# Last matrix product of an attention and two-layer kernel: 1280 of 2304 tokens by Strassen's seven products

## The chip, the cores and the metric

The kernel runs on one core of a Trainium2 chip. The metric is the device time of one execution in microseconds (us). Its engines are named as in the profile: PE (TensorE, the matrix unit; PEld are its weight loads), DVE (VectorE), ACT (ScalarE), POOL (GpSimd) and SP (SyncE, which here only issues the DMA transfers, in one queue and in order).

## The reference

```python
def reference(**kw):
    attn_out = _attn_ref(**attn_kwargs)          # 4 x 8 heads, 576 positions, 64 wide, causal
    x = attn_out.transpose(0, 2, 1, 3).reshape(2304, 512)
    x = _moe_ref(x=x, **moe_kwargs)              # 512 -> 2048 -> 512, leaky ReLU
    return _moe2_ref(x=x, **moe2_kwargs)

def _moe2_ref(x, w_in, w_out):
    h = x @ w_in                                 # 2304 x 512 @ 512 x 2048
    g = h * np.clip(h + 3.0, 0.0, 6.0) / 6.0
    return (g @ w_out).astype(np.float32)        # 2304 x 2048 @ 2048 x 512
```

The change concerns the last line alone: out = g @ w_out for 2304 tokens.

## The kernel before

The program is one long stream of matmuls on PE in stages: attention, the first pair of products (`w_in1`, `w_out1`), the product with `w_in2`, and the product with `w_out2`. Each fp32 factor is split into a high part, rounded to a narrower format that PE reads, and a low part that holds the rest (`split`: ACT copies the high part, line 160; DVE subtracts it, line 161). A product of two factors is then three matmuls: high by high, high by low, low by high.

The product with `w_in2` (line 879) already uses Strassen's form with seven products (the table `FORMS`). It runs over four groups of 576 tokens and eight steps j per group, and writes g to the HBM tensor `g_d` (named `g_scratch` in the profile), with 2048 rows (features) and 2304 columns (tokens).

The last stage (line 1042) reads g back in blocks of 512 tokens: four blocks of 512 and one of 256. For each of the 16 chunks f of 128 features it has a tile `gr` with two chunks (one DMA, line 1032, four buffers), the split of one chunk into `gh` and `gl` (three buffers each), and for each of the block's 128-token tiles three matmuls: gh or gl is the stationary factor (128 by 128), and the chunk of `w_out2` (`wo2[f]`, 512 columns) is the moving one. So a chunk takes 12 matmuls of 512 columns, a block 192. The sum over the chunks stays in one PSUM bank for each token tile; ACT scales it by 1/6 into `ot` (line 1052), and SP stores it.

The weights of this stage come in as 64-bit numbers that must be turned into fp32 on the chip first. `to_f32` does that for one chunk of 512 columns in five operations that depend on each other: ACT line 142, POOL line 144, POOL line 147, DVE line 152, DVE line 155. `split` then makes `wo` (ACT line 160, DVE line 161). `split_out` calls both, through two small buffers (`Spare`, the two halves of the tile `wo51`). Raw weights and results lie in the memory of `w_in2` pieces that are no longer needed (`places`). During the `w_in2` stage, `split_out` is called as soon as a raw chunk is there; the rest are called in the first block of the last stage, one for every second chunk.

The order on each engine is set when the program is built: a scheduler places the instructions by their priority, and each engine then goes through its own list strictly in order. An instruction whose data is late holds up all that stands behind it on that engine.

Of the kernel before, what the change touches and what calls it, by code (L numbers as in the profile page):

```python
# [61 lines left out]
def attention_moe_moe(ctx, tc, qt, kt, kq2, kqs, vs4, vp, s, w_in1, w_out1, alpha, w_in2, w_out2, out):  # L62
# [33 lines left out]
    def stage(**kw):  # L96
        roles.update(kw)
# [153 lines left out]
    def rows_of(p, n):  # L251

        out_, end = [], p + n
        while p < end:
            if p < B * NA:
                b, r = divmod(p, NA)
                m, t = min(end - p, NA - r), b * S + r
            else:
                b, r = divmod(p - B * NA, NQB)
                m, t = min(end - p, NQB - r), b * S + NA + r  # L260
            out_.append((t, m))
            p += m
        return out_
# [684 lines left out]
    wo2, outs = [], []  # L948

    places = []  # L950
    for j in range(4):
# [2 lines left out]
            places.append((f"wo{j - 1}1", j))  # L954
    places += [("wo31", 3), ("wo11", 3)]

    def load_out(f):

        t = wp.tile([P, CH, 2], U32, tag=places[f][0], name="wraw")
# [18 lines left out]
    with ExitStack() as ph2:  # L978
        cv = Spare()
        m5s = wp.tile([P, 2, NX2], F32, tag="wo71", name="m5")  # L980
        m2 = ph2.enter_context(tc.tile_pool(name="moe2", bufs=2))
        xbs = ExitStack()
        xb = xbs.enter_context(tc.tile_pool(name="xb", bufs=1))
        stage(a=[6, 1, 2], b=[0, 4, 5], c=[7, 3])
        xs[1] = load_x(xb, 1)
        last = None
        for i, (g, j) in enumerate(order):
            if i in (1, 3, 5):
                with tc.high_priority(offset=WLP):
# [28 lines left out]
        stage(o=[2, 5, 7, 0, 6, 3, 4, 1])
        NB2 = 512
        GC = 2  # L1020
        blocks = [(t0, min(NB2, NT - t0)) for t0 in range(0, NT, NB2)]
        for bi, (t0, n) in enumerate(blocks):
            ntt = n // P
            op = [bank("o") for i in range(ntt)]
            for f in range(FC):
                if bi == 0 and f < 2:
                    load_out(len(outs))
                if bi == 0 and len(wo2) < FC and f % 2 == 0:
                    split_out(len(wo2))
                if f % GC == 0:  # L1030
                    gr = gp.tile([P, GC, NB2], F32, tag="gr", bufs=4, name="gr")
                    nc.sync.dma_start(
                        gr[:, :, :n], g_d[f * P : (f + GC) * P, t0 : t0 + n].rearrange("(k p) t -> p k t", p=P)
                    )
                gh = gp.tile([P, NB2], F32R, tag="gh", bufs=3, name="gh2")
                gl = gp.tile([P, NB2], F32R, tag="gl", bufs=3, name="gl2")
                split(gh[:, :n], gl[:, :n], gr[:, f % GC, :n])
                wh, wl = wo2[f]
                for i in range(ntt):
                    tsl = slice(i * P, (i + 1) * P)  # L1040
                    for lt, r in ((gh, wh), (gh, wl), (gl, wh)):
                        nc.tensor.matmul(  # L1042
                            op[i], lt[:, tsl], r, start=(f == 0 and r is wh and lt is gh), stop=(f == FC - 1 and lt is gl)
                        )
            for i in range(ntt):
                ot = stg.tile([P, DM], F32, tag="yt", name="ot")
                halves = 2 if bi == len(blocks) - 1 else 1
                w = DM // halves
                for c in range(halves):
                    cols = slice(c * w, (c + 1) * w)  # L1050
                    if c == 0:
                        nc.scalar.activation(ot[:, cols], op[i][:, cols], AF.Copy, scale=1.0 / 6.0)
                    else:
                        nc.vector.tensor_scalar(ot[:, cols], op[i][:, cols], 1.0 / 6.0, 0.0, op0=ALU.mult, op1=ALU.add)
                    at = 0
                    for t, m in rows_of(t0 + i * P, P):
                        nc.sync.dma_start(out[t : t + m, cols], ot[at : at + m, cols])
                        at += m
# [37 lines left out]
```

## Time and profile before

| | |
|---|---|
| time, median of 3 runs | 1000.36 us (999.53 to 1003.92) |
| the profiled execution's own time | 1005.35 us |
| its span (first to last instruction) | 1003.6 us |
| PE busy | 980.6 us (98%) |
| DVE, ACT, POOL busy | 613.7, 632.2, 439.6 us |
| last matmul of the `w_in2` product ends, last stage alone on PE | about 812.7 us |
| last matmul of the last stage ends | about 999.0 us |

A row of the profile says which engine ran which line on which tile, for how long, and what ended the idle time before it. Matmuls are pipelined, so a row's duration for one matmul is longer than the distance to the next; distances between starts are what add up.

### The profile page before, as it was taken

To read this page: it belongs to the slowest core of one execution; us is meant where nothing else is said; L and a number is where in the kernel's file an instruction comes from. 1 tells how busy PE (TensorE), PEld (TensorE's weight loads), DVE (VectorE), ACT (ScalarE), POOL (GpSimd) and SP (SyncE) were. 2 spreads that over 40 slices of the span, in tenths; PEclk is the share of its full clock that TensorE was granted. 3 is DMA by queue.
4 is the path that set the end of the run, shared out by engine and by line. 5 is a ranking of instruction groups with operands and counts; after the bars stand their busy time and mean duration, and the time that the engine had idled before them with its cause. 6 is when DMAs were issued, how large, how long until landed. Compare 5 with 4: busy or idle time off the path is not lost.

```text
span 1003.6 us, 18109 instructions
## 1 busy us (share of the span) xinstructions
PE 980.6 (98%) x6218; PEld 880.8 (88%) x6218; DVE 613.7 (61%) x1504; ACT 632.2 (63%) x1434; POOL 439.6 (44%) x587
## 2 busy tenths in 40 slices
PE   8789999999999999999999999999999999999998
PEld 5568788999999998998998888999999988888886
DVE  5778885466666666766563895886658774222222
ACT  6568778678768778778764664766656653232322
POOL 5654666667666666666642763542202230000000
PEclk9779999999999999999999999999999999999999
DMA  6990014113122222213104421524248843443422
GB/s 212 300 361 1 24 30 128 45 46 91 52 76 74 58 69 83 67 52 97 52 14 153 122 94 63 194 107 150 111 158 289 280 153 116 116 147 86 145 62 85
DMA packets 60436, 114.47 MB, mean 114 GB/s; under 512 B 6056, under 2 KB 22744, under 8 KB 60344
## 3 DMA queue, kind: packets, MB, share of 16 engines
q1 hardware_dynamic: 60344, 113.32, 34.9%
q8 instruction: 49, 0.80, 0.3%
q14 instruction: 43, 0.35, 0.1%
HBM read 84.84 MB, written 28.46 MB: 113 GB/s over the span
## 4 chain that ended last, share of the span: by engine, by line
PE 92%; ACT 3%; DVE 2%; issue 1%; DMA 1%; POOL 1%; SPq 0%; DVEq 0%; POOLq 0%; ACTq 0%
PE h L248 20%; PE y L675 20%; PE o L1042 20%; PE a L879 10%; PE b L879 5%; PE s L410 4%; PE pv L472 4%; PE pt L447 4%; PE c L879 2%; PE s L322 1%; PE pv L603 1%; PE pt L593 1%; PE h L534 1%; DMA wraw<-in_w_in 1%; DMA gr<-g_scratch 1%
## 5 line engine op out<-in xcount | busy, mean ns | idle before, releaser
L248 PE MATMUL h<-xhi,wi 128*128 128x256 f32 (+1 forms) x896 | 228.3, 323 | 2.8 <-DVE gt L698 1.5
L1042 PE MATMUL o<-wo,gh 128*128 128x512 f32 x576 | 174.7, 389 | 0.0
L248 PEld LDWEIGHTS h<-xhi,wi 128*128 128x128 f32 x896 | 157.4, 192 | 16.4 <-DVE gt L698 1.9
L675 PE MATMUL y<-gh,wo 128*128 128x256 f32 (+1 forms) x896 | 162.0, 315 | 0.0
L248 PE MATMUL h<-xlo,wi 128*128 128x256 f32 (+1 forms) x448 | 143.7, 321 | 0.0
L675 PEld LDWEIGHTS y<-gh,wo 128*128 128x128 f32 x896 | 133.8, 190 | 11.2 <-ACT gh L701 0.4
L161 DVE TENSOR_TENSOR gl<-gr,gh 128x512 fp32r<-128x512 f32 (+1 forms) x80 | 51.1, 640 | 126.6 <-ACT gh L160 111.9
L1042 PEld LDWEIGHTS o<-wo,gh 128*128 128x128 f32 x576 | 107.9, 188 | 22.1
L160 ACT ACTIVATE gh<-gr 128x512 fp32r<-128x512 f32 (+1 forms) x80 | 46.8, 588 | 112.4 <-PE o L1042 109.7
L879 PE MATMUL a<-x,wc 128*128 128x288 f32 x768 | 113.2, 295 | 0.7 <-ACT z L886 0.7
L144 POOL TENSOR_SCALAR wcv<-wcv 128x512 f32<-128x512 f32 x64 | 47.7, 752 | 146.5 <-ACT wcv L142 142.4
L1042 PE MATMUL o<-wo,gl 128*128 128x512 f32 x288 | 109.5, 389 | 0.0
L879 PEld LDWEIGHTS a<-x,wc 128*128 128x128 f32 x768 | 106.0, 188 | 1.5 <-ACT z L886 1.2
L675 PE MATMUL y<-gl,wo 128*128 128x256 f32 (+1 forms) x448 | 91.6, 317 | 0.0
L248 PEld LDWEIGHTS h<-xlo,wi 128*128 128x128 f32 x448 | 86.3, 193 | 5.9
L422 POOL TENSOR_SCALAR t<-t,rec 128x384 f32<-128x384 f32 (+2 forms) x96 | 65.6, 686 | 57.3 <-DVE rec L421 32.9
L413 DVE CUSTOM_DVE_ANT_0 t<-s,mask 128x384 f32<-128x384 f32 (+2 forms) x96 | 53.4, 562 | 56.4 <-PE pt L447 34.4
L698 DVE SCALAR_TENSOR_TENSOR gt<-gt,beta,h 128x256 f32<-128x256 f32 (+1 forms) x112 | 61.7, 552 | 34.0 <-ACT gt L697 32.8
L418 ACT ACTIVATE t<-t,m 128x384 f32<-128x384 f32 (+2 forms) x96 | 67.2, 700 | 17.2 <-DVE m L413 15.8
L675 PEld LDWEIGHTS y<-gl,wo 128*128 128x128 f32 x448 | 69.7, 190 | 6.0 <-issue 0.2
L702 POOL TENSOR_TENSOR gl<-gt,gh 128x256 fp32r<-128x256 f32 x80 | 59.3, 743 | 31.4 <-ACT gh L701 29.5
L701 ACT ACTIVATE gh<-gt 128x256 fp32r<-128x256 f32 (+1 forms) x112 | 53.1, 477 | 29.5 <-DVE gt L698 27.9
(136 smaller groups left out, 2014.2 us busy)
## 6 DMA issues: line engine op xcount, KB each, us to landing
g_scratch<-gt SPq DMA_DIRECT2D x64, 288.0 KB
wraw<-in_w_in SPq DMA_DIRECT2D x32, 512.0 KB
wraw<-in_w_out SPq DMA_DIRECT2D x32, 512.0 KB
gr<-g_scratch SPq DMA_DIRECT2D x32, 512.0 KB
kraw<-in_kt SPq DMA_DIRECT2D x32, 288.0 KB
qraw<-in_qt SPq DMA_DIRECT2D x32, 160.0 KB
vraw<-in_vp SPq DMA_DIRECT2D x32, 160.0 KB
y_scratch<-yt SPq DMA_DIRECT2D x18, 256.0 KB
```

The source lines that it names most:

```text
L144: keep(nc.gpsimd.tensor_scalar(cf, cf, W_MOST, -W_MOST, op0=ALU.min, op1=ALU.max))
L161: keep(nc.vector.tensor_tensor(lo, of, hi.bitcast(F32), op=ALU.subtract))
L248: nc.tensor.matmul(dst, lt, r, start=first and i == 0, stop=last and i == len(terms) - 1)
L413: nc.vector.tensor_tensor_reduce(t[:n, a:e], sc[:n, : e - a], mask[:n, MASK + n - (e - a) :][:, : e - a] if e == w else mask[:n, : e - a], ...
L418: nc.scalar.activation(t[:n, :w], t[:n, :w], AF.Exp, bias=m[-1][:n], scale=-1.0, accum_out=den[:n])
L422: nc.gpsimd.tensor_scalar(t[:n, :w], t[:n, :w], rec[:n], 1.0, op0=ALU.mult, op1=ALU.mult)
L675: nc.tensor.matmul(ys[dc // per][:, o : o + n], which[:, dc * P : (dc + 1) * P], gg, start=(f == 0 and which is wl and dc % per == 0), sto ...
L698: nc.vector.scalar_tensor_tensor(gt, gt, beta[:, f : f + 1], hp[:, :n], op0=ALU.mult, op1=ALU.add)
L701: nc.scalar.activation(gh, gt, AF.Copy)
L702: (nc.vector if n == 512 else nc.gpsimd).tensor_tensor(gl, gt, gh.bitcast(F32), op=ALU.subtract)
L879: nc.tensor.matmul(dst[:, :NX2], lt, r, start=first and n == 0, stop=n == len(terms) - 1, skip_group_check=not first,)
L1042: nc.tensor.matmul(op[i], lt[:, tsl], r, start=(f == 0 and r is wh and lt is gh), stop=(f == FC - 1 and lt is gl))
```

## The change

The last stage is cut in two. The first 1024 tokens (two blocks of 512) go on as before, three buffers for `gr` in place of four, and the chunks are taken in the order 0, 8, 1, 9, ... (`chunks`), so that the two halves of the feature dimension come in pairs j. The other 1280 tokens are five blocks of 256 tokens. For them the product of each pair (2 by 128 tokens, 2 by 128 features, 2 by 256 columns) is made by Strassen's seven products instead of eight: 7 times 3 matmuls of 256 columns for each of the eight j. A block has four steps (`steps`, two j each).

What that needs besides matmuls:

- `make_forms(j)`, once for each j, placed in the two plain blocks: four differences of weights on DVE (line 1058, 256 columns each), split into new tiles `wf2` (two times ACT line 160 and DVE line 161, 512 columns). They need the whole fp32 weights. For j from 4 to 7 `split_out` now writes the converted weights straight into a kept tile (`direct`, through `Half`); for j from 0 to 3 DVE adds the high and low parts again (line 1054, two times 512 columns).
- `left_forms`, once for each of the 20 steps: two DMAs of 256 KB into `gq` (two buffers, line 1072), four sums and differences on DVE (lines 180 to 183, 256 columns each), and the split of `gq` (1024 columns) into `ga` and of the sums (768 columns) into `gs`. It is called one step ahead.
- `close`, once for each block: two copies on ACT, five operations on DVE (line 1104), two on POOL (lines 1110 and 1111), and the stores.

The kept tiles for j = 4 to 7 lie in memory that the last step of the `w_in2` product still uses (`slots[NJ + j]`), and only eight chunks of `w_out2` instead of all that are there are converted during that stage (`FC // 2`).

```diff
+    wo2, outs = {}, []
+    chunks = [j + h * NJ for j in range(NJ) for h in range(2)]
+    slots = [f"{nm}{j}{i}" for j in range(4, NU) for nm in ("wi", "wo") for i in range(2)]
+    slots.append(slots.pop(slots.index("wo51")))
+    direct = {}
...
+    def split_out(k):
+
+        f = chunks[k]
+        pool = cv
+        if k >= FC // 2:
+            j = f % NJ
+            if j not in direct:
+                direct[j] = wp.tile([P, 2, CH], U32, tag=slots[NJ + j], name="wf")
+            pool = Half(direct[j][:, f // NJ])
+        (cf,) = to_f32([outs[k]], pool, "wcv", 2, lambda ins: ins, (False,))
...
-                if len(wo2) < len(outs) - 1:
+                if len(wo2) < min(len(outs) - 1, FC // 2):
...
+        def make_forms(j):
+
+            if j in direct:
+                wf = direct[j].bitcast(F32)
+            else:
+                wf = gp.tile([P, 2, CH], F32, tag="wf", bufs=1, name="wf")
+                for h in range(2):
+                    hi, lo = wo2[j + h * NJ]
+                    nc.vector.tensor_tensor(wf[:, h], hi.bitcast(F32), lo.bitcast(F32), op=ALU.add)
+            tt = fp.tile([P, 4, ND], F32, tag="s", name="tt")
+            b11, b12, b21, b22 = (wf[:, h, c * ND : (c + 1) * ND] for h in range(2) for c in range(2))
+            for dst, x, y in ((0, b12, b11), (1, b22, tt[:, 0]), (2, b22, b12), (3, b21, tt[:, 1])):
+                nc.vector.tensor_tensor(tt[:, dst], x, y, op=ALU.subtract)
...
+        def left_forms(t0, jp):
+
+            gq = fp.tile([P, 2, 2, NS], F32, tag="gq", name="gq")
+            for h in range(2):
+                c = (h * NJ + 2 * jp) * P
+                nc.sync.dma_start(gq[:, h], g_d[c : c + 2 * P, t0 : t0 + NS].rearrange("(j p) t -> p j t", p=P))
+            sf = fp.tile([P, 3, 2, P], F32, tag="s", name="sf")
+            quads = [gq[:, h, :, m * P : (m + 1) * P] for h in range(2) for m in range(2)]
+            s_forms(nc.vector, *quads, [sf[:, i] for i in range(3)])
+            ga = fp.tile([P, 2, 2, 2, NS], F32R, tag="ga", name="ga")
+            split(ga[:, 0], ga[:, 1], gq)
+            gs = fp.tile([P, 2, 3, 2, P], F32R, tag="gs", name="gs")
+            split(gs[:, 0], gs[:, 1], sf)
...
+        ORDER = (1, 6, 5, 7, 2, 3, 4)
...
+        made = {(0, 6): 0, (0, 11): 1, (1, 0): 2, (1, 3): 3, (1, 5): 4, (1, 7): 5, (1, 9): 6, (1, 11): 7}
...
+                if (bi, k) in made:
+                    make_forms(made[bi, k])
+                if k % GC == 0:
+                    gr = gp.tile([P, GC, NB2], F32, tag="gr", bufs=3, name="gr")
...
+        for at, (t0, jp) in enumerate(steps):
+            if at + 1 < len(steps):
+                ahead.append(left_forms(*steps[at + 1]))
+            of = ahead.pop(0)
...
+                for k, i in enumerate(ORDER):
+                    a, b = FORMS[i - 1]
+                    (ah, al), (bh, bl) = of(a, jj), forms[j][b]
+                    for x, (lt, r) in enumerate(((ah, bh), (ah, bl), (al, bh))):
+                        tc.keep_in_program_order(
+                            nc.tensor.matmul(
+                                acc[i], lt, r, start=(j == 0 and x == 0 and k % 2 == 0),
```

How the lists of the engines change shows best at three places.

The first is on DVE, in the first plain block, up to the ninth chunk's weights, `wo_10920` in the changed kernel (in the kernel before, the ninth chunk's are `wo_10754`). The names: `wcv` and `wf` are weights under conversion, `gl2` the low part of a chunk of g, `tt` differences of weights, `wf2` their split. Before, the rows from the last conversion of chunks 8 and 9 on:

```order
L152 SCALAR_TENSOR_TENSOR wcv_8671<-wcv_8671,wraw_10453 128x512 [waits Pool_49]
L152 SCALAR_TENSOR_TENSOR wcv_8671<-wcv_8671,wraw_10455 128x512 [waits DMAHW7_49,Pool_49]
L155 SCALAR_TENSOR_TENSOR wcv_8671<-wraw_10453,wcv_8671 128x512 [waits DVE_49]
L155 SCALAR_TENSOR_TENSOR wcv_8671<-wraw_10455,wcv_8671 128x512 [waits DVE_49]
L161 TENSOR_TENSOR wo_10754<-wcv_8671,wo_10754 128x512 [waits Activation_49]
L893 SCALAR_TENSOR_TENSOR gt_10843<-gt_10843,a_10757 128x288 [waits Activation_49]
L161 TENSOR_TENSOR wo_10824<-wcv_8671,wo_10824 128x512 [waits Activation_49]
L161 TENSOR_TENSOR gl2_10998<-gr_10979,gh2_10997 128x512 [waits PE_49,Activation_49]
L889 TENSOR_TENSOR m5_8672<-a_10827,m5_8672 128x288 [waits PE_49]
```

Now, the last rows before the ninth chunk's weights are whole:

```order
L152 SCALAR_TENSOR_TENSOR wf_11199<-wf_11199,wraw_10912 128x512 [waits DMAHW0_49,Pool_49]
L161 TENSOR_TENSOR gl2_11154<-gr_11151,gh2_11153 128x512 [waits DMAHW2_49,PE_49,Activation_49]
L1058 TENSOR_TENSOR tt_11172<-wf_11169,tt_11172 128x256 [waits DVE_49]
L155 SCALAR_TENSOR_TENSOR wf_10914<-wraw_10453,wf_10914 128x512 [waits DVE_49]
L155 SCALAR_TENSOR_TENSOR wf_10914<-wraw_10455,wf_10914 128x512 [waits DVE_49]
L155 SCALAR_TENSOR_TENSOR wf_11199<-wraw_10912,wf_11199 128x512 [waits DVE_49]
L161 TENSOR_TENSOR wo_11148<-wf_11100,wo_11148 128x512 [waits Activation_49]
L1058 TENSOR_TENSOR tt_11172<-wf_11169,tt_11172 128x256 [waits DVE_49]
L161 TENSOR_TENSOR wf2_11177<-tt_11172,wf2_11177 128x512 [waits Activation_49]
L161 TENSOR_TENSOR wo_10920<-wf_10914,wo_10920 128x512 [waits Activation_49]
```

Before, `wo_10754` stands ahead of the last gate rows of the `w_in2` product (the next row of line 889 reads `a_10827`, that product's last step). Now the low part of `wo_10920` stands 32 rows behind that product's last DVE row (line 893 on `a_10811`), after the conversions of the other seven kept chunks and the weight differences of the first two j, and `gl2_11154`, a tile of the eleventh chunk, ahead of it.

The second place is PE, where the eighth chunk ends and the ninth begins. Before and now:

```order
L1042 MATMUL o_10924<-wo_10684,gh2_11081 128x512 x2
L1042 MATMUL o_10924<-wo_10684,gl2_11082 128x512
L1042 MATMUL o_10921<-wo_10754,gh2_11107 128x512 [waits Activation_49]
L1042 MATMUL o_10921<-wo_10754,gh2_11107 128x512
L1042 MATMUL o_10921<-wo_10754,gl2_11108 128x512 [waits DVE_49]
```

```order
L1145 MATMUL o_10911<-wo_10684,gl2_11085 128x512
L1145 MATMUL o_10908<-wo_10920,gh2_11111 128x512 [waits Activation_49]
L1145 MATMUL o_10909<-wo_10920,gh2_11111 128x512
L1145 MATMUL o_10910<-wo_10920,gh2_11111 128x512
L1145 MATMUL o_10911<-wo_10920,gh2_11111 128x512
L1145 MATMUL o_10908<-wo_10920,gh2_11111 128x512 [waits DVE_49]
```

The ninth chunk's first four matmuls now need the high part of `wo_10920` from ACT, and the fifth its low part from DVE; before, the waits there were for g alone.

The third place is one step of the Strassen blocks, which has nothing like it before: DVE's rows, and SP's two rows for the buffer that `ga_12038` gives free (`gq_12142` takes the memory of `gq_12030`; its first DMA waits on DVE).

```order
L161 TENSOR_TENSOR ga_12038<-gq_12030,ga_12038 128x1024 [waits Activation_49]
L181 TENSOR_TENSOR sf_12089<-sf_12089,gq_12086 128x256 [waits DVE_49]
L182 TENSOR_TENSOR gq_12086<-gq_12086 128x2x128
L183 TENSOR_TENSOR sf_12089<-gq_12086,sf_12089 128x256 [waits DVE_49]
L161 TENSOR_TENSOR gs_12097<-sf_12089,gs_12097 128x768 [waits Activation_49]
L180 TENSOR_TENSOR sf_12145<-gq_12142 128x256 [waits DMAHW1_49,DMAHW0_49]
L161 TENSOR_TENSOR ga_12094<-gq_12086,ga_12094 128x1024 [waits Activation_49]
```

```order
L1072 DMA gq_12142<-g_scratch 128x2x256 [waits DMAHW5_49,DMAHW4_49,DVE_49]
L1072 DMA gq_12142<-g_scratch 128x2x256
```

So between the rows of `ga` of two steps stands one row, line 180, that needs the DMA which the earlier of the two lets start.

## Rows read from the trace of the kernel before

**Rows 1.** The page: busy time, share of the span, instructions.

```profile
PE 980.6 (98%) x6218; PEld 880.8 (88%) x6218; DVE 613.7 (61%) x1504; ACT 632.2 (63%) x1434; POOL 439.6 (44%) x587
```

**Rows 2.** Chain that ended last, from 805 us: start, length, what.

```profile
812.07 0.79 PE a L879 x6
812.86 186.15 PE o L1042 x821
...
999.03 0.39 ACT ot L1052
```

**Rows 3.** Stretches: busy us and count of PE, PEld, DVE, ACT, POOL; clock; DMA.

```profile
812.70:999.03 186.33, 186.33 (x824) 154.15 (x822) 56.62 (x91) 57.91 (x101) 5.47 (x8) 1.00 0.37 112
```

**Rows 4.** PE in order of time, 256-column matmuls: start, us, operation, count.

```profile
199.83 1.00 PE L675 MATMUL y<-gh,wo 128*128 128x256 f32 x7
200.67 0.64 PE L675 MATMUL y<-gl,wo 128*128 128x256 f32 x4
201.15 0.28 PE L248 MATMUL h<-xhi,wi 128*128 128x256 f32 x1
```

**Rows 5.** DVE in order of time, around the last `w_in2` matmul.

```profile
809.88 0.76 DVE L893 SCALAR_TENSOR_TENSOR gt<-gt,z 128x576 f32<-128x576 f32 x1 [0.40 <-ACT gt L892]
...
813.60 0.45 DVE L893 SCALAR_TENSOR_TENSOR gt<-gt,a 128x288 f32<-128x288 f32 x1
813.97 0.69 DVE L161 TENSOR_TENSOR wo<-wcv,wo 128x512 fp32r<-128x512 f32 x1
...
820.79 1.29 DVE L152 SCALAR_TENSOR_TENSOR wcv<-wcv,wraw 128x512 uint32<-128x512 uint32 x2
821.99 1.29 DVE L155 SCALAR_TENSOR_TENSOR wcv<-wraw,wcv 128x512 uint32<-128x512 uint32 x2
823.20 0.69 DVE L161 TENSOR_TENSOR gl<-gr,gh 128x512 fp32r<-128x512 f32 x1
```

**Rows 6.** Groups by shape from 600 us: busy, mean ns, idle before.

```profile
L161 DVE TENSOR_TENSOR x<-yr,x 128x1152 fp32r<-128x1152 f32 x6 | 8.1, 1352 | 4.5 <-ACT x L160 4.5
L161 DVE TENSOR_TENSOR gl<-gr,gh 128x256 fp32r<-128x256 f32 x16 | 6.7, 425 | 18.5 <-ACT gh L160 10.1 <-PE o L1042 8.4
L161 DVE TENSOR_TENSOR x<-yt,x 128x864 fp32r<-128x864 f32 x6 | 6.3, 1050 | 0.0
```

**Rows 7.** ACT and POOL in order of time: gate, conversion and split.

```profile
812.90 0.51 ACT L892 ACTIVATE gt<-a,three 128x288 f32<-128x288 f32 x1 [1.75 <-PE a L879]
...
815.17 0.66 ACT L142 ACTIVATE wcv<-wraw 128x512 f32<-128x512 f32 x1
...
822.77 1.23 ACT L160 ACTIVATE wo<-wcv 128x512 fp32r<-128x512 f32 x2
...
815.91 0.63 POOL L144 TENSOR_SCALAR wcv<-wcv 128x512 f32<-128x512 f32 x1 [5.92 <-ACT wcv L142]
817.55 1.72 POOL L147 TENSOR_SCALAR wraw<-wcv 128x512 f32<-128x512 f32 x2
```

**Rows 8.** PE waits and the granted clock (last figure but two).

```profile
48.15:54.97 6.82, 4.42 (x18) 3.34 (x19) 6.72 (x12) 2.66 (x7) 1.36 (x2) 0.50 0.98 268
54.97:65.21 10.24, 7.46 (x42) 5.05 (x40) 7.74 (x33) 7.29 (x25) 5.21 (x10) 1.00 1.04 407
170.00:180.00 10.00, 8.44 (x70) 8.03 (x69) 4.07 (x16) 9.78 (x30) 9.41 (x16) 1.00 0.45 125
...
50.55 0.69 PE L603 MATMUL pv<-pT,vraw 128*64 128x256 f32 x2 [4.11 <-DVE pT L597]
174.65 0.39 PE L248 MATMUL h<-xhi,wi 128*128 128x256 f32 x1 [1.54 <-DVE gt L698]
```

**Rows 9.** GB/s in 40 slices of 2.6 us from a 256 KB `gr` issue, then 3.5 us from a 512 KB one.

```profile
GB/s 0 0 0 0 0 0 0 0 0 0 0 0 0 0 0 79 95 110 110 126 79 79 110 189 221 236 347 362 378 347 299 299 174 110 126 110 32 16 0 0
GB/s 0 0 0 0 0 0 0 0 0 0 0 117 117 140 140 23 140 47 70 187 140 187 281 304 421 374 421 421 398 398 398 398 328 258 164 70 47 0 0 0
```

**Rows 10.** Chain at the start of the `gr` loads: landing of the first of four.

```profile
783.46 5.23 DMA gr<-g_scratch
```

More of the change, by code (lines that the diff above doesn't have):

```diff
@@ L955, in attention_moe_moe, with load_out, __init__, tile @@
     places += [("wo31", 3), ("wo11", 3)]
-    def load_out(f):
-        t = wp.tile([P, CH, 2], U32, tag=places[f][0], name="wraw")
+    def load_out(k):
+        f = chunks[k]
+        t = wp.tile([P, CH, 2], U32, tag=places[k][0], name="wraw")
         tc.keep_in_program_order(nc.sync.dma_start(t.rearrange("p f t -> p (f t)"), w_out2[f * P : (f + 1) * P, :].bitcast(U32)))
         outs.append(t)
-    def split_out(f):
-        (cf,) = to_f32([outs[f]], cv, "wcv", 2, lambda ins: ins, (False,))
-        t = wp.tile([P, 2, CH], F32R, tag=places[f][0], name="wo")
+    class Half:
+        def __init__(self, of):
+            self.of = of
+        def tile(self, *args, **kw):
+            return self.of
+    def split_out(k):
+        f = chunks[k]
+        pool = cv
[5 more added lines that the diff above has]
+        (cf,) = to_f32([outs[k]], pool, "wcv", 2, lambda ins: ins, (False,))
+        t = wp.tile([P, 2, CH], F32R, tag=places[k][0], name="wo")
         split(t[:, 0], t[:, 1], cf)
-        wo2.append((t[:, 0], t[:, 1]))
+        wo2[f] = (t[:, 0], t[:, 1])
     A1, B1 = 3, 4
@@ L1017, in attention_moe_moe @@
         right.close()
[L1018 to L1023, printed above, removed]
+        fp = late.enter_context(tc.tile_pool(name="forms", bufs=2, side="right"))
+        NB2, NS, GC = 512, 256, 2
+        ND = DM // 2
+        plain = (0, NB2)
+        rest = range(2 * NB2, NT, NS)
+        forms = []
+        def make_forms(j):
[10 more added lines that the diff above has]
+                nc.vector.tensor_tensor(tt[:, dst], x, y, op=ALU.subtract)
+            t = []
+            for i in range(2):
+                hl = wp.tile([P, 2, 2, ND], F32R, tag=slots[2 * j + i], name="wf2")
+                split(hl[:, 0], hl[:, 1], tt[:, 2 * i : 2 * i + 2])
+                t += [(hl[:, 0, c], hl[:, 1, c]) for c in range(2)]
+            q = [tuple(x[:, c * ND : (c + 1) * ND] for x in wo2[j + h * NJ]) for h in range(2) for c in range(2)]
+            forms.append([q[0], t[2], q[2], q[3], t[0], t[1], t[3]])
@@ new lines, in left_forms, with of @@
+        def left_forms(t0, jp):
[10 more added lines that the diff above has]
+            split(gs[:, 0], gs[:, 1], sf)
+            def of(a, jj):
+                if a < 4:
+                    h, m = divmod(a, 2)
+                    return tuple(ga[:, x, h, jj, m * P : (m + 1) * P] for x in range(2))
+                return tuple(gs[:, x, a - 4, jj] for x in range(2))
+            return of
@@ new lines, in attention_moe_moe, with store_rows, close, add @@
+        ORDER = (1, 6, 5, 7, 2, 3, 4)
+        def store_rows(t0, ot):
+            at = 0
+            for t, m in rows_of(t0, P):
+                nc.sync.dma_start(out[t : t + m, :], ot[at : at + m])
+                at += m
+        def close(t0, acc):
+            e = m2.tile([P, 2, ND], F32, tag="z", bufs=2, name="e")
+            u = m2.tile([P, 2, ND], F32, tag="gt", bufs=3, name="u")
+            o = [stg.tile([P, DM], F32, tag="yt", name="ot") for _ in range(2)]
+            def add(dst, i, to):
+                nc.vector.scalar_tensor_tensor(dst, acc[i], 1.0 / 6.0, to, op0=ALU.mult, op1=ALU.add)
+            nc.scalar.activation(e[:, 0], acc[1], AF.Copy, scale=1.0 / 6.0)
+            add(u[:, 0], 6, e[:, 0])
+            nc.scalar.activation(e[:, 1], acc[5], AF.Copy, scale=1.0 / 6.0)
+            add(u[:, 1], 7, u[:, 0])
+            nc.gpsimd.tensor_tensor(o[0][:, ND:], u[:, 0], e[:, 1], op=ALU.add)
+            nc.gpsimd.tensor_tensor(o[1][:, ND:], u[:, 1], e[:, 1], op=ALU.add)
+            add(o[0][:, :ND], 2, e[:, 0])
+            add(o[0][:, ND:], 3, o[0][:, ND:])
+            store_rows(t0, o[0])
+            add(o[1][:, :ND], 4, u[:, 1])
+            store_rows(t0 + P, o[1])
@@ L1024, in attention_moe_moe @@
+        steps = [(t0, jp) for t0 in rest for jp in range(NJ // 2)]
+        ahead = []
+        stage(o=[2, 5, 7, 0, 6, 3, 4, 1], m=[2, 5, 7, 0, 6, 3, 4, 1])
+        made = {(0, 6): 0, (0, 11): 1, (1, 0): 2, (1, 3): 3, (1, 5): 4, (1, 7): 5, (1, 9): 6, (1, 11): 7}
+        for bi, t0 in enumerate(plain):
+            ntt = NB2 // P
             op = [bank("o") for i in range(ntt)]
-            for f in range(FC):
-                if bi == 0 and f < 2:
+            for k, f in enumerate(chunks):
+                if bi == 0 and k < 2:
@@ L1027, in attention_moe_moe @@
                     load_out(len(outs))
-                if bi == 0 and len(wo2) < FC and f % 2 == 0:
+                if bi == 0 and len(wo2) < FC and k % 2 == 0:
                     split_out(len(wo2))
[L1030 to L1034, printed above, removed]
+                if (bi, k) in made:
+                    make_forms(made[bi, k])
@@ L1035, in attention_moe_moe @@
+                if k % GC == 0:
+                    gr = gp.tile([P, GC, NB2], F32, tag="gr", bufs=3, name="gr")
+                    nc.sync.dma_start(gr, g_d.rearrange("(h j p) t -> j p h t", h=2, p=P)[f, :, :, t0 : t0 + NB2])
                 gh = gp.tile([P, NB2], F32R, tag="gh", bufs=3, name="gh2")
                 gl = gp.tile([P, NB2], F32R, tag="gl", bufs=3, name="gl2")
-                split(gh[:, :n], gl[:, :n], gr[:, f % GC, :n])
+                split(gh, gl, gr[:, k % GC])
                 wh, wl = wo2[f]
+                if bi == 1 and k == FC - 4:
+                    ahead.append(left_forms(*steps[0]))
+                    fp.tile([P, LINE], F32, tag="line", bufs=1, name="line")
@@ L1042, in attention_moe_moe @@
                         nc.tensor.matmul(
-                            op[i], lt[:, tsl], r, start=(f == 0 and r is wh and lt is gh), stop=(f == FC - 1 and lt is gl)
+                            op[i], lt[:, tsl], r, start=(k == 0 and r is wh and lt is gh), stop=(k == FC - 1 and lt is gl)
                         )
@@ L1046, in attention_moe_moe @@
                 ot = stg.tile([P, DM], F32, tag="yt", name="ot")
[L1047 to L1058, printed above, removed]
+                nc.scalar.activation(ot, op[i], AF.Copy, scale=1.0 / 6.0)
+                store_rows(t0 + i * P, ot)
+        for at, (t0, jp) in enumerate(steps):
+            if at + 1 < len(steps):
+                ahead.append(left_forms(*steps[at + 1]))
+            of = ahead.pop(0)
+            if jp == 0:
+                if at:
+                    close(t0 - NS, acc)
+                banks = [bank("m") for _ in range(4)]
+                acc = {i: banks[k // 2][:, k % 2 * ND : (k % 2 + 1) * ND] for k, i in enumerate(ORDER)}
+            for jj in range(2):
+                j = 2 * jp + jj
+                for k, i in enumerate(ORDER):
[5 more added lines that the diff above has]
+                                acc[i], lt, r, start=(j == 0 and x == 0 and k % 2 == 0),
+                                stop=(j == NJ - 1 and x == 2 and (k % 2 == 1 or k == 6)),
+                            )
+                        )
+        close(t0, acc)
         late.close()
```

1 line of the change is left out of this document (removed).

## The prediction

> **What bounds the kernel now.** First the page's totals: PE is busy 980.6 of the 1003.6 us of the span, 98%, and no other engine is above 63% [rows 1]. Then the chain of waits, read at its end: the last matmuls of the `w_in2` product (six in 0.79 us from 812.07) are followed by one piece of 186.15 us, 821 matmuls of line 1042, without a wait in it, and then by 4 to 5 us of scaling and storing [rows 2]. The stretch table says the same of this stage: PE 186.33 of 186.33 us at the full clock (1.00), DVE 56.62, ACT 57.91 [rows 3]. So the changed stage is bound by the number and size of its matmuls, and DVE and ACT have two thirds of their time free there. One matmul of 512 columns takes 186.15 / 821 = 226.7 ns from start to start. What one of 256 columns takes is seen in an earlier stage, where eleven in a row start between 199.83 and 201.15: 120.0 ns [rows 4]. That is 6.6 ns more than half of 226.7, so a matmul has a part that doesn't shrink with its columns.
>
> **What goes and what comes on PE.** The 1280 tokens took 2.5 blocks of 192 matmuls, 480 x 226.7 ns = 108.8 us. Now five blocks of 8 x 7 x 3 = 168, 840 x 120.0 ns = 100.8 us. Seven products for eight would make 95.2 us if small matmuls cost in proportion; the fixed part eats 5.6 of it. PE saves 8.0 us, which all counts, since nothing else ends later there now. The outer ends are 113.4 ns (half of 226.7; saves 13.5) and the 0.79 / 6 = 131.7 ns of 288 columns [rows 2] (loses 1.8); the row of the same shape decides, so I keep it within 2 ns, 6.3 to 9.7.
>
> The Trainium skill, page "TensorE: Matmul & The Clock Gate", section "Back-to-back issue gap", gives N / 2.4 + 2.5 ns for an isolated matmul: 215.8 and 109.2 ns, and as an estimate from it a saving of 103.6 - 91.7 = 11.9 us. Both shapes have rows here, 11 ns above it each, so the rows decide and the rule's larger gain gets no chance.
>
> **What comes on DVE, in the plain blocks.** The weight differences, their splits and the sums of lines 1054 and 1058 go into a time when DVE has room over the whole stage [rows 3], but the list is strict, and here I expect the loss. Let T be the end of the last `w_in2` matmul (812.7 before). The order of DVE shows that the ninth chunk's weights `wo_10920` are finished only after all kept chunks are converted and the first two j have their differences, and PE can't go past its ninth chunk without them.
>
> When does DVE reach them? Ahead of that list stand `gl2_11013`, which waits for PE to free a `gh` buffer 14 matmuls of 512 columns and the last six before T (3.97 us before it), then ACT's copy (0.62) [rows 7], the subtraction at 0.60 and the gate of 576 columns, 0.76 [rows 5]: it ends about T - 1.9. From there to the low part of `wo_10920` the list has 42 instructions: 33 of 512 columns, 8 of 256 and one gate of 288. Distances between starts: 0.60 for 512 (two in a row from 820.79 to 821.99, two more to 823.20), 0.37 for 288 (813.60 to 813.97) [rows 5], and between these by columns 0.34 for 256. That is 19.8 + 2.7 + 0.4 = 22.9 us, T + 21.0. DVE finds no wait in it: I followed ACT (copies at 0.62) and POOL (0.63 and 0.86 each) [rows 7] along, and they are ahead of it throughout.
>
> PE after T has 10 matmuls of the fourth chunk and 48 of the next four: 58 x 0.2267 = 13.15 us. Then the ninth chunk's first four matmuls wait for the high part, which ACT can make once DVE's line 155 is done, 3.4 us before T + 21.0, so at about T + 18.2; they take 0.9 in the wait for the low part. PE loses 21.0 - 13.15 - 0.9 = 6.9 us, in two pieces of about 5.1 and 1.8. After that PE's next needs come 2.72 us (12 matmuls) apart and DVE stays 1 to 3 us ahead of them. The two sums of line 1054 that stand ahead of T among the gates (1.2 us) lie in DVE's waits for ACT, such as the 0.40 ahead of the gate [rows 5], and fewer conversions stand there than before; without that cover they would add up to 1.2. The bounds: if DVE took the ninth chunk first, its chain would be 0.51 + 0.66 + 0.63 + 0.86 + 0.60 + 0.60 + 0.62 + 0.60 = 5.1 us behind T, and nothing would be lost; with full durations (0.69, 0.425, 0.45 [rows 5, 6]) in place of distances the list takes 26.6 us and the loss is 10.6. I take 6.9, since back-to-back rows are what the list will be.
>
> The stall can be paid twice, through the clock. In the trace, a wait of PE of 4.11 us lies in a stretch at 0.50 (1.2 GHz), which lasts 4.4 us beyond PE's return at 50.55; a wait of 1.54 us at 174.65 lies in one at 1.00 [rows 8]. The expected wait of 5.1 is nearer to the first. 4.4 us at half speed lose 2.2 us, but part of them falls into the second wait; bounds 0 to 2.2, I take 1.1.
>
> **What comes in the Strassen blocks.** A step is 42 matmuls, 5.04 us. DVE has four sums (0.34), the split of 1024 columns and that of 768. By the rows of 864 and 1152 columns an element costs (1352 - 1050) / 288 = 1.05 ns, so 1.22 and 0.95 us, 0.09 less from start to start [rows 6]: 1.36 + 1.13 + 0.86 = 3.35 us a step, and with five operations at 0.34 for `close` 15.1 of a block's 20.2 us. It fits, and costs nothing while it does. ACT copies the same columns without the sums, and POOL's two operations for `close` have the whole next block.
>
> The tighter thing is a loop: the subtraction for `ga` frees its `gq` buffer, SP loads the step after next, and the next `ga` stands behind line 180, which reads that load. So a step can't be shorter than landing + 0.34 + 1.13 + some 0.1 for handing over. For the landing of two DMAs of 256 KB there is no row. One of 256 KB lands 2.47 us after its issue, data flowing from 0.98 on, and one of 512 KB, the same bytes, 3.24 us [rows 9]. I take 3.24: 4.8 us, under 5.04, nothing lost. The bounds are 2.47 (4.0 us) and, one after the other, 2.47 + 1.49 = 3.96 (5.5 us), or 5.23 as in the crowd of four loads and stores at 783.46 [rows 10] (6.8 us).
>
> The end stays: two operations of about 0.4 on DVE and two stores, as before one on ACT, one on DVE and four half-size stores. The stores of `close` and the fewer `gr` buffers lie beside matmuls: a `gr` load lands in 3.24 us and serves two chunks, 5.4 us.
>
> **The sum**, against the profiled execution's own span: -8.0 + 6.9 + 1.1 = 0. That execution took 1005.35 us, 5.0 more than the median of the runs shown, so I apply the difference to the median: 1000.4 us. Within 0.5% (5 us) counts as no change, about what a measurement of this kernel can tell.
>
> **The rivals.**
> - The stall doesn't come, or is short, because DVE's rows are quicker or something ahead of them starts earlier. For it: DVE is idle for 130 of the stage's 186 us [rows 3], and PE has not waited there before. Against: the strict list. Then 1000.4 - 8.0 = 992.4. With a stall under 3 us the result is faster.
> - The buffer loop is longer than a step, slower than before. For it: the first load after a crowd took 5.23 us, and 1 KB pieces are half of what `gr` has. Against: DMA engines are busy 37% there [rows 3]. It decides from a landing of 3.5 us on; at 3.96 it adds 0.49 x 19 steps less some 2.4 us of lead, 6.9, on top of the forecast: 1007.3.
> - DVE runs the long list at full durations, because each waits for the one before: 10.6 for 6.9, clock 2.2: 1005.2, at the edge of slower.
>
> **How the numbers follow.** Forecast, a stall that eats the gain: 0.53, with a range of its own of 996 to 1004. No or short stall: 0.22, faster. Buffer loop: 0.14, slower. Long list: 0.11, half of it slower. So faster 0.22, same 0.59, slower 0.19. The range 993 to 1007 leaves out about half of the first and of the second rival.
>
> **What would show it.** PE of the changed kernel: a wait of about 5 us some 13 us after the last matmul of line 879, released by ACT `wo`, and a second of 1 to 2 us released by DVE `wo`, four matmuls later. DVE without idle time for 20 us before. The granted clock at 0.50 in one stretch there. Matmuls of line 1168 at 120 ns, 840 in 101 us, no wait of PE for `ga`; if PE waits there for DVE each step, with DVE waiting for DMA `gq`, the loop has won. Wrong would be the forecast if the first wait is missing, or if line 1168 takes over 104 us.

## The result and the profile after

The changed kernel takes 1011.83 us (median of 6 runs, 1010.71 to 1015.95) beside 1001.32 us for the kernel before (6 runs, 999.53 to 1003.92): a ratio of 1.0108, 95% interval 1.0084 to 1.0132. It is slower by 10.5 us, where 1000.4 and a range of 993 to 1007 were predicted. The profiled execution took 1015.95 us, the longest of the six, with a span of 1013.9.

The totals of the page, which answer to [rows 1]: PE has lost 7.5 us of busy time and still the span has grown, so what came is waiting, and work at half the clock, which counts as busy.

```profile
PE 973.1 (96%) x6578; PEld 888.9 (88%) x6578; DVE 691.6 (68%) x1655; ACT 648.5 (64%) x1442; POOL 450.0 (44%) x597
```

The waits of PE in the last stage (engine, line, who released it: us in total, times, longest). Before there was none [rows 2]. Now there are two kinds: one long wait for converted weights, and four for `ga` in the Strassen blocks.

```profile
PE o L1145 <- ACT wo L160: 8.4, 1, 8.4
PE m L1168 <- DVE ga L161: 5.1, 4, 1.7
PE o L1145 <- DVE wo L161: 0.5, 1, 0.5
PE o L1145 <- DVE gl L161: 0.4, 2, 0.2
```

PE in order of time around the long wait. The last `w_in2` matmul of the changed kernel ends at T = 808.74 (six from 807.95, the next matmul at 808.74). PE reaches the ninth chunk at 822.90, T + 14.2, and stands until 831.43.

```profile
821.88 1.19 PE L1145 MATMUL o<-wo,gl 128*128 128x512 f32 x4 [0.16 <-DVE gl L161]
831.43 2.08 PE L1145 MATMUL o<-wo,gh 128*128 128x512 f32 x4 [8.36 <-ACT wo L160]
834.05 0.79 PE L1145 MATMUL o<-wo,gh 128*128 128x512 f32 x1 [0.55 <-DVE wo L161]
834.64 0.63 PE L1145 MATMUL o<-wo,gl 128*128 128x512 f32 x1
835.07 0.63 PE L1145 MATMUL o<-wo,gh 128*128 128x512 f32 x1
```

From 834.64 on a matmul takes 430 ns from start to start, not 226.7. The stretch table shows why (columns as in [rows 3], the granted clock is the last figure but two): half clock (0.50) for 10.24 us, which began while PE stood, and full clock (1.00) afterwards.

```profile
827.67:837.91 10.24, 5.93 (x13) 4.25 (x14) 10.24 (x20) 4.12 (x7) 0.00 (x0) 0.50 0.16 51
840.00:850.00 10.00, 10.00 (x45) 8.28 (x45) 10.00 (x24) 4.63 (x8) 0.00 (x0) 1.00 0.36 108
```

Now VectorE and GpSimd ahead of that wait, in order of time; they answer to [rows 5, 7].

```profile
806.73 3.16 DVE L152 SCALAR_TENSOR_TENSOR wf<-wf,wraw 128x512 uint32<-128x512 uint32 x3
...
813.22 0.68 DVE L155 SCALAR_TENSOR_TENSOR wf<-wraw,wf 128x512 uint32<-128x512 uint32 x1
...
816.48 1.12 DVE L152 SCALAR_TENSOR_TENSOR wf<-wf,wraw 128x512 uint32<-128x512 uint32 x1
817.52 1.12 DVE L161 TENSOR_TENSOR gl<-gr,gh 128x512 fp32r<-128x512 f32 x1
818.56 1.12 DVE L161 TENSOR_TENSOR wo<-wf,wo 128x512 fp32r<-128x512 f32 x1
...
819.94 0.68 DVE L161 TENSOR_TENSOR wf<-tt,wf 128x512 fp32r<-128x512 f32 x1
...
833.32 1.88 DVE L161 TENSOR_TENSOR wo<-wf,wo 128x512 fp32r<-128x512 f32 x3
```

```profile
806.67 1.64 POOL L144 TENSOR_SCALAR wf<-wf 128x512 f32<-128x512 f32 x2 [2.87 <-ACT wf L142]
...
810.08 1.91 POOL L144 TENSOR_SCALAR wf<-wf 128x512 f32<-128x512 f32 x2 [0.72 <-ACT wf L142]
812.07 0.98 POOL L147 TENSOR_SCALAR wraw<-wf 128x512 f32<-128x512 f32 x1
815.28 0.74 POOL L144 TENSOR_SCALAR wf<-wf 128x512 f32<-128x512 f32 x1 [2.23 <-ACT wf L142]
816.10 3.06 POOL L147 TENSOR_SCALAR wraw<-wf 128x512 f32<-128x512 f32 x3
```

The list begins at 806.73, T - 2.0, and the ninth chunk's low part (the first of the three at 833.32) is done at 833.92, T + 25.2, without idle time between: 27.2 us. Operations of the same shape take 1.12 us while GpSimd works (816.10 to 819.16) and 0.68 when it doesn't. GpSimd slows down too: 1.02 us for one of line 147, where two take 1.27 beside an idle VectorE (the kernel before, 827.06).

Last, a turn of the chain in the Strassen blocks (start, length, what). It runs from a landing of `gq`, here a late one, over the first sum and `ga` to the next load, here an undisturbed one. The 0.35 us that the view puts on line 181 are time in which SyncE issues the first of the two loads; the landing counts from the second. The row below the chain shows two such issues, 0.87 us together, one turn earlier.

```profile
931.04 4.21 DMA gq<-g_scratch
...
935.35 0.43 DVE sf L180
935.77 1.14 DVE ga L161
936.91 0.35 DVE sf L181
937.26 0.04 SPq L1072
937.30 0.06 issue
937.35 2.88 DMA gq<-g_scratch
```

```profile
930.64 0.87 SPq L1072 DMA_DIRECT2D gq<-g_scratch  x2
```

### The profile page after: what moved, and what is told of

It reads as the page before. It is cut to its first block, busy times and chain, and to the rows that moved or that the text cites. A ratio compares the mean times of both kernels' runs of the same rounds, so it can differ in the third digit from the quotient of the medians.

```text
span 1013.9 us, 19017 instructions
## 1 busy us (share of the span) xinstructions
PE 973.1 (96%) x6578; PEld 888.9 (88%) x6578; DVE 691.6 (68%) x1655; ACT 648.5 (64%) x1442; POOL 450.0 (44%) x597
## 4 chain that ended last, share of the span: by engine, by line
PE 80%; DMA 8%; DVE 7%; ACT 2%; issue 2%; SPq 1%; POOL 0%; DVEq 0%; POOLq 0%; ACTq 0%
PE y L675 20%; PE h L248 19%; PE a L879 10%; PE o L1145 7%; PE b L879 5%; PE s L410 4%; DMA gq<-g_scratch 4%; PE pv L472 4%; PE pt L447 4%; PE m L1168 3%; PE c L879 2%; DVE ga L161 2%; DMA wraw<-in_w_out 2%; PE s L322 1%; DMA vraw<-in_vs 1%
## 5 line engine op out<-in xcount | busy, mean ns | idle before, releaser
L144 POOL TENSOR_SCALAR wcv<-wcv 128x512 f32<-128x512 f32 x56 | 42.1, 760 | 112.2 <-ACT wcv L142 109.2
L1145 PE MATMUL o<-wo,gh 128*128 128x512 f32 x256 | 78.5, 399 | 8.9 <-ACT wo L160 8.4
L1110 POOL TENSOR_TENSOR ot<-u,e 128x256 f32<-128x256 f32 x5 | 3.7, 750 | 183.9 <-DVE u L1104 165.4
L383 POOL TENSOR_TENSOR ks<-kraw,ks 64x576 fp32r<-64x576 f32 (+1 forms) x40 | 52.5, 1313 | 40.8 <-issue 33.4
L1145 PEld LDWEIGHTS o<-wo,gh 128*128 128x128 f32 x256 | 49.2, 193 | 20.2 <-ACT wo L160 8.8
L697 ACT ACTIVATE gt<-h 128x256 f32<-128x256 f32 (+1 forms) x112 | 48.8, 440 | 20.1 <-PE h L248 14.3
```

Of the source, the lines that this page charges most:

```text
L383: nc.gpsimd.tensor_tensor(ks[D:P], kraw[D:P], ks[D:P].bitcast(F32), op=ALU.subtract)
L697: nc.scalar.activation(gt, hp[:, :n], AF.Relu, scale=-1.0)
L1145: nc.tensor.matmul(op[i], lt[:, tsl], r, start=(k == 0 and r is wh and lt is gh), stop=(k == FC - 1 and lt is gl))
```

## The experiments

Every kernel is the changed one with one edit; ratios are to the kernel before, run beside it. The reference point is the changed kernel's 1.0108.

**1. No late conversions.**

```diff
-        if k >= FC // 2: ... pool = Half(direct[j][:, f // NJ])
-        (cf,) = to_f32([outs[k]], pool, ...)
+        (cf,) = to_f32([outs[k]], cv, ...)
-                if len(wo2) < min(len(outs) - 1, FC // 2):
+                if len(wo2) < len(outs) - 1:
```

> All chunks are converted as in the kernel before (one by one as their loads land, into the small two-part buffer), none late; the sums of line 1054 are then made for all eight j. Theory (the late conversions make the stall): PE's 8.4 and 0.5 us waits for wo go, and with them the stretch at half clock from 827.67 to 837.91, 10.2 + 3.2 us in all by the trace of the changed kernel; the waits for ga in the Strassen blocks stay, 5.8 us. Time about 1011.8 - 13.4 = 998.4. Rival (the differences and sums on VectorE are the burden, not the late conversions): a wait of 4 us or more stays in the first plain block, and the time is 1004 or more.

Ratio 1.0021 (1.0004 to 1.0038): 8.7 us came back, not 13.4. The 8.4 us wait went, but another came at the fifteenth chunk (126 matmuls after T), with 3.41 us at half clock behind it:

```profile
PE m L1162 <- DVE ga L161: 2.8, 3, 1.5
PE o L1139 <- ACT wo L160: 2.3, 1, 2.3
```

So the time lies between the theory's and the rival's. The late conversions cost most of it; what makes the new wait stays open. (The waits for `ga` were shorter here too, which the edit doesn't aim at.)

**2. The kept tiles in slots that come free first.**

```diff
-  direct[j] = wp.tile([P, 2, CH], U32, tag=slots[NJ + j], name="wf")
+  direct[j] = wp.tile([P, 2, CH], U32, tag=slots[j - 4], name="wf")
-  hl = wp.tile([P, 2, 2, ND], F32R, tag=slots[2 * j + i], name="wf2")
+  hl = wp.tile([P, 2, 2, ND], F32R, tag=slots[(2 * j + 4 + i) % 16], name="wf2")
```

> The kept float tiles of j = 4 to 7 lie in the weight slots that come free first instead of last, the differences go to the others; the rest is as in the changed kernel, the number of instructions too. Theory (the stall comes from the slot of the ninth chunk, which is freed at the last w_in2 matmul, and from what then stands in VectorE's list): the ninth chunk's low part is done ahead of that matmul, the stall and its half clock go, about 998.4 us. Rival (VectorE has too much to do in that stretch wherever it starts): the wait moves ahead of the last w_in2 matmul or to a later chunk, at least 5 us in all, 1004 or more.

Ratio 0.9981 (0.9965 to 0.9997). PE has no wait and no half clock in the plain blocks. In the Strassen blocks two waits for `ga` are left; ahead of T a wait of 1.0 us for a gate is new, of the sort that the rival expects but far under its 5 us:

```profile
PE m L1168 <- DVE ga L161: 1.5, 2, 0.8
PE a L879 <- DVE gt L893: 1.0, 1, 1.0
...
```

The same work begins 15 us ahead of T instead of 2 and the time falls by 12.7 us: it was the slot, freed at the last `w_in2` matmul, that put the work on the path. A part of the 12.7 is the shorter waits for `ga`, which the edit doesn't aim at.

**3. Late conversions without GpSimd.**

```diff
-  for c, cf, high, low, by in ops:
+  for c, cf, high, low, by in ops if pooled else ():
       keep(nc.gpsimd.tensor_scalar(...))    # both operations; pooled is k < FC // 2
```

> In the late conversions (chunks 8 to 15 of the order) GpSimd's two operations of each chunk are left out, the clamp and the sign: the weights of these chunks come out wrong. Theory (an operation of VectorE with two inputs in SBUF that runs beside one of GpSimd takes 1.02 us from start to start for 0.60): the ten slow rows of the list are back at 0.60, the list ends 4.3 us sooner, PE's wait of 8.4 becomes about 4.1, time about 1007. Rival (the long rows come from something else, such as each waiting for the result of the one before): rows of 1.02 to 1.09 us stay, and the time changes by less than 1 us.

Ratio 0.9955 (0.9939 to 0.9971). No row of that shape is above 0.69 us now, as the theory says (groups by shape, 800 to 836: busy, mean ns):

```profile
L161 DVE TENSOR_TENSOR gl<-gr,gh 128x512 fp32r<-128x512 f32 x13 | 8.9, 686 | 0.0
...
L152 DVE SCALAR_TENSOR_TENSOR wf<-wf,wraw 128x512 uint32<-128x512 uint32 x6 | 4.0, 688 | 0.0
```

But the whole stall went, 15 us and not 4.3. The expectation missed that with a shorter chain the order of VectorE changes too: the first late conversions now stand ahead of T. The rows hold, the time is no price of GpSimd's part.

**4. Three `gq` buffers.**

```diff
-  gq = fp.tile([P, 2, 2, NS], F32, tag="gq", name="gq")
+  gq = fp.tile([P, 2, 2, NS], F32, tag="gq", bufs=3, name="gq")
```

> gq has three buffers for two. Theory (the loop landing of gq, sum of line 180, subtraction for ga, issue of the next load is longer than a step, with landings of 4.2 to 5.0 us in every third step): PE's waits for ga in the Strassen blocks, 5.8 us above a matmul's own time, go nearly all, VectorE no longer waits for DMA gq, and the dip of the clock at 988 may go too (1.7): 1004 to 1006 us. Rival (VectorE and ScalarE with the block's closing operations set the pace): PE's waits for ga stay at 4 us or more, 1010 or more.

Ratio 1.0061 (1.0039 to 1.0083), 4.7 us less, where 6 to 8 were expected. PE has no wait for `ga` any more; the waits of the stall are as they were (8.4, 0.6 and 0.4). The stretch table over the Strassen blocks: PE without a gap, 840 matmuls in 100.7 us, while ACT and DVE do the same work as before.

```profile
903.40:1004.20 100.80, 100.80 (x841) 100.74 (x839) 71.17 (x123) 37.33 (x48) 6.41 (x9) 1.00 0.35 109
```

That settles the loop, and it confirms the gain: 100.7 for 108.8 us.

**5. Slots and buffers together.**

> The slots of the second experiment and the third gq buffer together. Theory (the change's gain on PE is 8.0 us, and the two things that ate it are the stall and the buffer loop): no wait of PE above its matmuls in the last stage; from the last w_in2 matmul to the last matmul 179.1 us (346 of 226.7 ns and 840 of 120.0 ns) against 186.3 in the kernel before; the end after the last matmul 0.1 to 0.9 longer. Time 6.3 to 7.2 us under that of the kernel before, a ratio of about 0.9935. Rival (the waits removed come back elsewhere, or another load lies behind the third buffer's): above 0.997.

995.42 us, ratio 0.9937 (0.9918 to 0.9955): faster than both kernels, and as expected. Plain and Strassen blocks run through (ahead of T two waits of some 0.5 us for gates are left):

```profile
810.20:887.58 77.38, 77.38 (x343) 63.85 (x342) 58.53 (x115) 34.35 (x58) 1.82 (x2) 1.00 0.47 146
887.58:988.40 100.82, 100.82 (x841) 100.74 (x839) 71.31 (x123) 37.35 (x48) 6.39 (x9) 1.00 0.35 109
```

The two repairs add up within the intervals, some 2 us to either side: 12.7 + 4.7 = 17.4 us alone, 17.1 together. That the two figures lie so close is partly luck, since experiment 2 already had fewer waits for `ga`.

**6. Differences behind the last late conversion.**

```diff
-  made = {(0, 6): 0, (0, 11): 1, (1, 0): 2, ...}
+  made = {(1, 0): 2, (1, 2): 3, (1, 4): 4, (1, 6): 5, (1, 8): 6, (1, 10): 7, (1, 12): 0, (1, 14): 1}
-  split(t[:, 0], t[:, 1], cf)
+  split(t[:, 0], t[:, 1], cf, tc.keep_in_program_order)    # late chunks; the differences too
```

The differences stand in the order in which they are made, so the products take those of other j; the work is the same.

> All differences and sums of the weights are put behind the last late conversion in VectorE's order, and made in the second plain block; the late conversions stay where they are. 5.7 us of differences, sums and their splits leave the list that ends in the ninth chunk's low part. Theory (PE waits for the length of that list): its waits for wo, 9.5 us in all, become 3.8; with a shorter stretch at half clock the time is 1004 to 1006. Rival (the chain ScalarE, GpSimd, VectorE of the conversions sets the end, and the differences only fill its gaps): waits for wo of 8 us or more, 1010 or more.

Ratio 1.0047 (1.0031 to 1.0063), and the waits for `wo` are 4.4 us for 8.9:

```profile
PE o L1145 <- ACT wo L160: 4.2, 1, 4.2
PE m L1168 <- DVE ga L161: 3.0, 4, 0.9
PE o L1145 <- DVE wo L161: 0.2, 1, 0.2
```

The list now has 28 operations of 512 columns and a gate. At their distances they take 17.2 us; with ten of them beside GpSimd at 0.43 more, 21.5; PE goes on 21.9 us after the list's start at 804.78. The theory holds, its 3.8 us a little short.

**7. GpSimd writes and reads nothing.**

```diff
-  nc.gpsimd.tensor_scalar(cf, cf, W_MOST, -W_MOST, op0=ALU.min, op1=ALU.max)
+  nc.gpsimd.memset(cf, 0.5)    # and memset(high, 0.0) for the second
```

> In the late conversions GpSimd's two operations of each chunk are replaced by two that write a constant into the same tile and read nothing: the weights of these chunks come out wrong. Theory (VectorE's second input and GpSimd's read share a way into SBUF): rows of VectorE beside GpSimd's stay at 0.68 us, 0.60 from start to start. Rival (any instruction of GpSimd slows VectorE): rows beside it take about 1.1 us as in the changed kernel.

One run, 999.2 us, too few for a verdict on the time; the order has moved as in the third. VectorE first, then GpSimd, in order of time (lines 161 and 147 of this kernel are 155 and 144 of the changed one):

```profile
811.15 0.69 DVE L161 SCALAR_TENSOR_TENSOR wf<-wraw,wf 128x512 uint32<-128x512 uint32 x1
...
818.21 0.69 DVE L161 SCALAR_TENSOR_TENSOR wf<-wraw,wf 128x512 uint32<-128x512 uint32 x1
```

```profile
811.35 0.53 POOL L147 MEMSET wf<- 128x512 f32 x1 [1.48 <-ACT wf L142]
...
818.16 0.53 POOL L147 MEMSET wf<- 128x512 f32 x1 [4.78 <-ACT wf L142]
```

Both run beside each other at their own speed, whichever starts first: between 799 and 820 us eleven operations of VectorE of this shape lie beside such a write, and none takes over 0.69 us. So it is GpSimd's reading that slows VectorE, as the theory says.

**8. `ga` ahead of the next sum, two buffers.**

```diff
-  split(ga[:, 0], ga[:, 1], gq)
+  split(ga[:, 0], ga[:, 1], gq, tc.keep_in_program_order)    # the sums and gs too
```

> Two gq buffers as in the changed kernel, but VectorE makes a step's sums, its ga and its gs before the next step's first sum. Theory (the loop is long because ga, which frees the buffer, stands behind the next step's sum, which waits for the next load): the load after next is issued some 4.4 us after the landing of its buffer's last load, two steps have 10.1 us for it, and PE's waits for ga fall from 5.8 to under 1.5 us: 1006 to 1008. Rival (with two buffers the loads are late in any order): 4 us or more of waits for ga stay, 1010 or more.

Ratio 1.0073 (1.0051 to 1.0094), 3.5 us less, where 4 to 6 were expected. PE's waits in the last stage are those of the stall (8.4, 0.6 and 0.2), with none for `ga`: the theory again, by the order and not by memory. Its interval reaches that of the changed kernel, so the exact gain stays open; the missing waits do not.

## Why the prediction was wrong

In the forecast's sum, -8.0 + 6.9 + 1.1 = 0, the gain held and three terms were too small: the list of VectorE (10.0 for 6.9), the clock (2.7 for 1.1) and the buffer loop (5.8 for nothing).

**The gain on PE: right.** 8.0 us by 120.0 ns a matmul. Experiments 4, 5 and 8 have 100.7 us for the 840. The larger gain, 11.9 us, did not come and had rightly been given no chance.

**The list of VectorE: the place right, the size wrong.** The wait came 14.2 us behind T (forecast 13.15; two short waits for `gl`, 0.7 us, are the most of the rest), released by ACT's `wo`, and the second four matmuls later by VectorE's. The list began at T - 2.0 (forecast T - 1.9, though its terms, -3.97 + 0.62 + 0.60 + 0.76, add up to -2.0). What failed is the step that set all 33 operations of 512 columns at 0.60 us, "back-to-back rows are what the list will be", after following GpSimd only as something to wait for. Ten operations of the list (nine of 512 columns, one of 256) lay beside GpSimd's reads and took 0.43 us more each: 22.9 + 4.3 = 27.2, which is what the trace has. PE lost 8.53 (8.76 from start to start, less a matmul's own 0.23), 0.75 (1.18 less 0.43 at half clock) and 0.71, together 10.0 us for 6.9. The upper bound of 10.6 held the size by another cause. Experiments 3 and 7 show the cause by rows; the Trainium skill's page "SBUF — State Buffer", section "Who interferes with whom", states it: a VectorE instruction with two inputs in SBUF contends with a GpSimd instruction that reads SBUF, not with one that only writes. The trace agrees in both halves. It was to be read beforehand: [rows 7] have 0.86 us for GpSimd beside VectorE and 0.63 alone, and further up in the trace of before a subtraction of line 161 takes 1.13 us for 0.69 beside this row of GpSimd:

```profile
652.51 1.13 DVE L161 TENSOR_TENSOR wc<-wcv,wc 128x512 fp32r<-128x512 f32 x1
```

```profile
652.48 0.61 POOL L144 TENSOR_SCALAR wcv<-wcv 128x512 f32<-128x512 f32 x1 [1.18 <-ACT wcv L142]
```

There GpSimd starts first and VectorE pays. At 817.46 a row of VectorE starts first, 0.09 us ahead of GpSimd's two of line 147 [rows 7], and keeps its own time; GpSimd's two take 1.72 us for the 1.27 that they take alone:

```profile
817.46 0.69 DVE L161 TENSOR_TENSOR gl<-gr,gh 128x512 fp32r<-128x512 f32 x1 [1.39 <-ACT gh L160]
```

```profile
827.06 1.27 POOL L147 TENSOR_SCALAR wraw<-wcv 128x512 f32<-128x512 f32 x2
```

So not every row in such company is slow: of 32 in the trace of before (512 columns, lines 152, 155 and 161, at least 0.3 us beside lines 144 and 147), 15 took less than 0.8 us. In the list of the changed kernel GpSimd's rows follow each other closely in three runs (806.67 to 809.36, 810.08 to 813.05, 815.28 to 819.16), and ten rows of VectorE paid.

**The clock: mis-sized.** 1.1 us was taken and 2.2 the bound. From 831.43 to 837.63 twelve matmuls took 6.2 us for 2.7; without the 0.75 of waiting, the half clock cost 2.7. In experiment 4, with the same stall, the stretch lasted 13.65 us and cost about 3.8. After a wait of 4.4 (experiment 6) or 2.5 us (experiment 1) it lasted 3.41. The row of [rows 8], after 4.11 us of waiting, was no measure for one twice as long.

**The Strassen blocks: the rival came true.** The forecast put a turn of the loop at 4.8 us and the cost at nothing; the rival, chance 0.14, had 6.9 on top of it, and 5.8 came (waits above a matmul's own time: 1.10, 1.54, 1.25, 1.90). An undisturbed landing was near the forecast, 2.9 to 3.1 us from the second issue for 3.24. What was left out is that SyncE issues the two loads one after the other: `ga` ends, and the second load leaves 0.44 us later, where 0.1 was set. With 0.10 + 0.42 + 1.14 + 0.44 + 3.05 an undisturbed turn takes 5.15 us for a step of 5.04. On top, about every third load was late (4.2 to 5.0 us): PE's waits end at 936.96, 953.71, 970.38 and 987.78, so three steps took 16.7 to 17.4 us for 15.1. An overrun of 0.11 us in each of 19 steps would come to 2.1 us, which the lead of some 2.4 us in the forecast would cover; so, as an estimate, it is the late loads that the waits come from, and the step that failed is the one value, 3.24, for every landing. The size differs between executions: in the five other traces with this loop unchanged (experiments 1, 2, 3, 6 and 7) the same waits come to 1.8 to 4.1 us, and experiments 4 and 8, which take them away, gain 4.7 and 3.5. VectorE's own work was no bound, as forecast: experiment 4 has it all in 100.7 us.

**The end: right.** From the start of the last matmul to the end 4.69 us, before 4.74.

The sum with the measured terms, -8.0 + 10.0 + 2.7 + 5.8 = 10.5, is as large as the measured difference of the medians, but that it fits so well is partly luck. In the two profiled executions PE takes 200.4 us from T to the start of its last matmul, where it took 186.1 in the kernel before; four more matmuls of 512 columns lie behind T, so the stage has grown by 13.4 us. The sum leaves out another stretch at half clock (988.09 to 991.50, 1.7 us) and 1.2 us in small pieces, such as 0.1 us in the matmul behind a wait. On the other side the changed kernel's execution was 3.1 us shorter ahead of T: the one before has two stretches of 3.41 us at half clock, at 382 and 464 us. All three begin 0.3 to 1.0 us after short waits of PE (1.7 us at 988; 0.8 and 0.3 to 0.5 us at the other two). The waits at 382 stand in the changed kernel's trace too, without half clock behind them, so whether such a stretch comes differs between executions; what decides it stays open.

## What to carry to other kernels

A list of operations on VectorE isn't priced by back-to-back rows alone: count those with two SBUF inputs that will lie beside reads of GpSimd. Here the one that started second paid, some 0.43 us; where GpSimd's rows follow each other closely, price VectorE's at the row that had such company, and take the back-to-back row as the lower bound. Where a loop runs over a buffer, add the issue of every DMA of the turn, and compare its length with the step by its slowest common turn, not by an undisturbed one; a forecast margin of 5% was none here, and one more buffer or one operation moved ahead took it all back. When a tile goes into memory that others free, the order of freeing decides when its work can start: the same conversions cost some 12 us or nothing.

## What was not expected of the hardware

Which `gq` loads are late is told by the DMA queues. In seven traces (the changed kernel, experiments 1 to 6) the Strassen blocks have 110 loads. 84 went without a 16 KB packet of the queue marked "instruction" beside them; their last data came 2.57 to 3.00 us after the second issue. Of 26 with one, 21 took 3.33 to 4.55 us; in the other five it came at the end of the data (in the changed kernel's, at 914.01, the landing was late all the same, 4.72 us). The queue table of the changed kernel from 931.0 to 935.3 us (the landing of 4.21) has such a packet, that from 937.3 to 940.3 (2.88) has none:

```profile
q1 hardware_dynamic: 544, 0.52, 39.3%
q8 instruction: 1, 0.02, 1.9%
q14 instruction: 1, 0.01, 0.4%
```

```profile
q1 hardware_dynamic: 544, 0.52, 55.6%
```

The packet of the other queue, q14, has 8 KB. It is not the cause: six of the 84 loads had one of these alone beside them and took 2.65 to 2.96 us.

In the Strassen blocks of the changed kernel the 16 KB packets come 15.2 to 18.4 us apart. The Trainium skill's page "Runtime: NRT & Kernel Launch", section "Instruction fetch mechanics", gives 16 KiB, 256 instructions, as the block in which an engine's program is loaded, and calls the cost of going from one to the next mostly hidden. As an estimate from it, a block is 128 matmuls with their weight loads: 15.4 us at 120 ns, about three steps, and 29.0 us at 226.7 ns. The traces agree with that: in the last stage of the kernel before, from 832 us on, the packets come 28.3 to 29.7 us apart. PE's own waits in the table above all have VectorE or ScalarE as releaser; it was a load of data beside the packet that came late, by some 0.6 to 1.8 us. That the two go together is shown; why stays open. The last stage before had no load with such a packet in its midst (three of 512 KB had one at their beginning or end, and were not late), so there was no row to read it from.
